# Attention's matmuls dealt out one by one from a template, on one Trainium2 core

## The chip, the core and the metric

The kernel runs on one NeuronCore of a Trainium2 chip. TensorE (PE in the profile) does the matrix products and the transpositions. Before each matmul it loads the stationary operand, a step that the profile keeps as an engine of its own (PEld). VectorE (DVE), ScalarE (ACT) and GpSimd (POOL) do the elementwise work. SyncE (SP) and ACT issue the DMAs. Each engine works through its instructions in a fixed order and waits on semaphores for the others. The metric is the device time of one execution in microseconds, lower is better.

## The reference

One transformer block in float32: x has 2048 rows of 1024. The attention has 32 heads of 32 columns and works on four segments of 512 rows; beside the causal softmax inside a segment it reads a memory M, z that sums up the earlier segments.

```python
for s in range(N):                                     # N = 4 segments of L = 512 rows
    qs, ks, vs = q[:, :, s], k[:, :, s], v[:, :, s]
    logits = jnp.einsum("bhqd,bhkd->bhqk", qs, ks) * scale + mask
    p = _softmax(logits, axis=-1)
    a_dot = jnp.einsum("bhqk,bhkd->bhqd", p, vs)
    pq = phi(qs)
    num = jnp.einsum("bhld,bhde->bhle", pq, M)
    den = jnp.einsum("bhld,bhd->bhl", pq, z)[..., None] + 1e-6
    o = g * (num / den) + (1.0 - g) * a_dot
    pk = phi(ks)
    M = M + jnp.einsum("bhld,bhle->bhde", pk, vs)
    z = z + jnp.einsum("bhld->bhd", pk)
...
h = x + _A_ref(_layernorm(x), ...)                     # the above, then times wo
h2 = h + _B_ref(_layernorm(h), ...)                    # gelu(y @ w1 + b1) @ w2 + b2, 3584 wide
```

## The kernel before

The rows are done in two halves of 1024. Each half runs the attention on two segments, then the product with `wo`, the second LayerNorm and the MLP. The MLP and all of its order are the same in both kernels.

Float32 accuracy is bought with split operands: each float32 value is a high part in fp32r and a low part (the rest), and a product is three matmuls, high by high, high by low and low by high. The low parts are made by subtractions on DVE and POOL.

**A unit** is one group of four heads (`g`, eight of them) in one segment (`sl`, two in a half): 16 units in a half. Its work on PE:

- The dense products: `kps`, `qps`, `vps`, each 8 chunks of 3 matmuls (L114 to L116), 72 matmuls with 128 columns of weights and 512 moving columns. The weights of a group are split by `weights` and `load_block`: the low part `wl` is a subtraction on POOL (L91).
- For each of its four heads: four score products `pqk` (L523, 128 to 512 moving columns), ten 128x128 transpositions `ppt` of the probabilities (L555), and eight products with the values, `po` (L575, 128 to 512 moving columns, only 64 columns of weights). I call these PV.
- The memory: transpositions `pkn`, `vn` and `pom` (four each), twelve products `pm` that read the memory (L386, 132 moving columns) and twelve products `pmm` that update it (L386, 128 columns). The first segment has no `pm` and `pom`, the last no `pmm` and `pkn`.

Between these stand DVE (the row minimum L524, the reciprocal L536, the low parts `ptl` L562), ACT (the exponential L532, the high parts `pth` L557) and POOL (the scaling of the probabilities `pr`, L539).

**What sets the order.** The program is written with generators. `dense` makes the dense products of one unit and yields after each chunk of three matmuls. `heads(prev)` makes the heads of the unit before, and `interleave` takes a step of the one and a step of the other. A head is a `slot` of six steps, written in `PLAN`: a letter is an operation and its digit a part, so `q1` is the score product of row block 1, `n0` the scaling of row blocks 0 and 1, `t0` the first group of four transpositions, `s0` its low parts, `a0` four PV matmuls, `o` the output. The letters work on three heads at a time: the present one (q, n), the one before (t, s) and the one before that (a, o, S).

The memory products wait in a list `small`. `one_small` takes one of them; it is called ahead of each transposition in `ptr` and ahead of most PV matmuls in `av`, so that a small product stands between two transpositions. The rest of a unit's memory work (`vn`, the filling of the list, `pom`) is in `late`, which runs in the next unit's dense part. A planner then takes this written order as priorities, and chooses each engine's final order from what it holds to be ready; in the MLP the written order is kept instead.

At the end of a half, the last unit's heads run beside the first `wo` products (`wo_first`), again by `interleave`, with the rates RA, RH and RS.

Of the kernel before, what the change touches and what calls it, by code (L numbers as in the profile page):

```python
# [16 lines left out]
P = 128  # L17
# [25 lines left out]
def build(tc, x, wq, wk, wv, wo, beta, w1, b1, w2, b2, out):  # L43
# [292 lines left out]
    def attention(half, first):  # L336
# [56 lines left out]
        def dense(g, sl, ws, u):  # L393
            s = 2 * half + sl
            behind = acts.pop("late", iter(()))
            kps = ws.pop("kps", None)
            if kps is None:
                kps = ps_dense("kps")
                for c in project(ws["k"], sl, "kps", kps):
                    if c >= 2:  # L400
                        next(behind, None)
                    yield
# [5 lines left out]
            for c in project(ws["q"], sl, "qps", qps):  # L408
                if c == 0:
                    nc.vector.tensor_tensor(kl, kps, raw(kh), op=ALU.subtract)  # L410
                    u["ks"] = stack(kh, kl, "ks", (0, 1, 0))
                if c == 2 and s < 3:
                    zc = ab.tile([P, 64], F32, name="zc", bufs=2)[:, 0:1]
                    pk = phi_sum(kparts, "pk", zc)
                next(behind, None)
                yield
# [4 lines left out]

            vps = ps_dense("vps")
            for c in project(ws["v"], sl, "vps", vps):
                if c == 0:
                    nc.vector.tensor_tensor(ql, qps, raw(qh), op=ALU.subtract)
                    u["qs"] = stack(qh, ql, "qs", (0, 0, 1))
                if s > 0:
                    if c == 2:
                        pq = phi_sum(qparts, "pq")
                    if c == 4:  # L430
                        while small:
                            one_small()
                        pqh, pql = tmpr("pqh"), tmpr("pql")
                        mzh = ab.tile([P, 256], F32R, name="mzh", bufs=1)[:, 0:132]
                        mzl = ab.tile([P, 256], F32R, name="mzl", bufs=1)[:, 0:132]
                        nc.scalar.copy(pqh, pq)
                        nc.vector.tensor_copy(mzh, MZ[:, g, :])
                        nc.gpsimd.tensor_tensor(mzl, MZ[:, g, :], raw(mzh), op=ALU.subtract)
                    if c == 5:
                        nc.gpsimd.tensor_tensor(pql, pq, raw(pqh), op=ALU.subtract)  # L440
                if c == 1 and s < 3:
                    pkn = ps_dense("pkn")
                    for i in range(4):
                        nc.tensor.transpose(pkn[:, i * P:(i + 1) * P], pk[:, i * P:(i + 1) * P], ident)
                    pkh, pkl = tmpr("pkh"), tmpr("pkl")
                    nc.scalar.copy(pkh, pkn)
                if c == 2 and s < 3:
                    nc.vector.tensor_tensor(pkl, pkn, raw(pkh), op=ALU.subtract)
                next(behind, None)
# [7 lines left out]
            def late():  # L457
                vn = ps_dense("vn")
                for c in range(4):
                    nc.tensor.transpose(vn[:, c * P:(c + 1) * P], vt[:, c * P:(c + 1) * P], ident)  # L460
# [3 lines left out]
                yield  # L464
                if s > 0:
                    om = tmp("om")

                    def memory(i2, ps):
                        pm = ps.rearrange("p (a b) -> p a b", a=2)
                        rg = ab.tile([P, 2, 32], F32, name="rg", bufs=2)[:, :, 0:4]  # L470
                        nc.vector.tensor_scalar(rg, pm[:, :, 128:132], DEN_EPS, None, op0=ALU.add)
                        nc.vector.reciprocal(rg, rg)
                        nc.vector.tensor_tensor(rg, rg, gate[:, 0:1, 4 * g:4 * g + 4].to_broadcast([P, 2, 4]), op=ALU.mult)
                        nc.vector.tensor_tensor(
                            om[:, i2 * 256:(i2 + 1) * 256].rearrange("p (a h e) -> p a h e", a=2, h=4),
                            pm[:, :, 0:128].rearrange("p a (h e) -> p a h e", h=4),
                            rg.unsqueeze(3).to_broadcast([P, 2, 4, DH]), op=ALU.mult)

                    for i2 in range(2):
                        smalls("pm", [(lambda ps, ii=ii: ps[:, 256 * ii:256 * ii + 132],  # L480
                                       pqh[:, (2 * i2 + ii) * P:(2 * i2 + ii + 1) * P],
                                       pql[:, (2 * i2 + ii) * P:(2 * i2 + ii + 1) * P], mzh, mzl, True, True)
                                      for ii in range(2)], partial(memory, i2))
                left = len(small)
                if s < 3:
                    def update(pmm):
                        for j in range(4):
                            b = slice(32 * j, 32 * j + 32)
                            nc.vector.tensor_tensor(MZ[b, g, b], pmm[b, b], MZ[b, g, b], op=ALU.add)
                        nc.vector.scalar_tensor_tensor(MZ[:, g, 128:132], hsel, zc, MZ[:, g, 128:132], op0=ALU.mult, op1=ALU.add)  # L490

                    smalls("pmm", [(lambda ps: ps[:, 0:P].rearrange("p (a b) -> p a b", a=4),
                                    pkh[:, c * P:(c + 1) * P], pkl[:, c * P:(c + 1) * P],
                                    vs[:, 4 * c:4 * c + 4, 0:32], vs[:, 4 * c:4 * c + 4, 32:64], c == 0, c == 3)
                                   for c in range(4)], update)
                total = len(small)
                while len(small) > total - left:
                    yield
                yield
                if s > 0:  # L500
                    pom = ps_dense("pom")
                    for i in range(4):
                        one_small()
                        nc.tensor.transpose(pom[:, i * P:(i + 1) * P], om[:, i * P:(i + 1) * P], ident)
                    nc.scalar.copy(omt, pom)  # L505
                while small:
                    yield
            for _ in behind:
                one_small()
            acts["late"] = late()  # L510
# [31 lines left out]
        def ptr(st, n):  # L542
            grp = ((0,), (1, 3), (2,))[n]
            if n == 0:
# [3 lines left out]
            ppt = psum.tile([P, 512], F32, tag="pt", name="ppt", bufs=2)  # L548
            base = koff[grp[0]]
            w = 0  # L550
            for jk in grp:
                for i in range(jk, 4):
                    one_small()
                    o = koff[jk] - base + (i - jk) * P
# [843 lines left out]
```

## Time and profile before

| | us |
|---|---|
| median of 3 runs (2356.2 to 2359.72) | 2358.24 |
| span of the profiled execution | 2354.0 |
| median less span (what lies around the instructions, and the difference of executions) | 4.2 |

| stretch of the span | what runs | PE busy |
|---|---|---|
| 0 to 60 us | the opening, first units | 46.27 of 60 |
| 60 to 530 us | attention of the first half | 455.27 of 470 |
| 950 to 1400 us | attention of the second half | 443.57 of 450 |
| the rest | `wo`, LayerNorm, MLP | not touched by the change beyond `wo_first` |

Matmuls are pipelined: the time given for one includes its way through the array, and the next starts before it ends. So a busy PE may still wait. How long a matmul really holds PE is read from the timeline, as the distance from its start to the start of the next. A matmul of 512 columns that follows another stands 0.23 us from the next. The timeline's columns are start, length, engine, line, operation, names, shape and count.

### The profile page before, as it was taken

The numbers are of one execution on the slowest core, as the hardware profiler recorded it, in microseconds if no ns is written. First come the engines' busy times: TensorE is split into PE (matmuls) and PEld (weight loads), VectorE is DVE, ScalarE is ACT, GpSimd is POOL, SyncE is SP. The second block draws the span as 40 slices with busy tenths as digits, with TensorE's granted clock in tenths as the row PEclk, the third lists the DMA queues.
The fourth block names the chain that finished last, engine by engine and source line by source line (L and its number), as shares of the span: only waits on it lengthen the run. The fifth ranks groups of instructions, "written<-read, shape, count | busy, mean of one in ns | idle before, by whom it ended". The sixth has DMA issues, their size and how long they took to land.

```text
span 2354.0 us, 35355 instructions
## 1 busy us (share of the span) xinstructions
PE 2288.6 (97%) x11769; PEld 1893.4 (80%) x11769; DVE 1575.9 (67%) x3334; ACT 1228.8 (52%) x2557; POOL 1058.4 (45%) x1037
## 2 busy tenths in 40 slices
PE   7999999999999999999999999999999999999999
PEld 6888888878878887888888877778887888888887
DVE  6777777776655565777777777564566676566753
ACT  5676776785453444777777776363343233222321
POOL 4444444445243442555555545252444564255430
PEclk9999999999999999999999999999999999999999
DMA  5333333345365654433333334466557976576762
GB/s 172 95 89 91 86 81 87 83 115 174 127 196 171 192 161 137 124 83 84 88 83 85 89 93 132 152 198 175 168 176 251 341 254 204 160 251 222 255 219 94
DMA packets 322719, 355.36 MB, mean 151 GB/s; under 512 B 26190, under 2 KB 218730, under 8 KB 322538
## 3 DMA queue, kind: packets, MB, share of 16 engines
q1 hardware_dynamic: 259370, 316.40, 44.7%
q10 hardware_dynamic: 63168, 36.71, 5.2%
q8 instruction: 93, 1.52, 0.3%
q14 instruction: 88, 0.72, 0.1%
HBM read 226.59 MB, written 76.09 MB: 129 GB/s over the span
## 4 chain that ended last, share of the span: by engine, by line
PE 73%; DVE 9%; ACT 7%; DMA 4%; POOL 3%; issue 3%; SPq 1%; ACTq 0%; POOLq 0%; DVEq 0%
PE po L1235 21%; PE bps L856 8%; PE dps L856 5%; PE ppt L555 5%; PE po L575 4%; PE cps L856 4%; PE pqk L523 3%; PE kps L114 2%; PE kps L115 2%; PE kps L116 2%; PE vps L114 2%; PE vps L115 2%; PE vps L116 2%; PE qps L114 2%; PE qps L115 2%
## 5 line engine op out<-in xcount | busy, mean ns | idle before, releaser
L539 POOL TENSOR_SCALAR pr<-pr,nm,gate 128x128 f32<-128x128 f32 (+3 forms) x512 | 320.9, 636 | 400.6 <-DVE nm L536 293.1
L532 ACT ACTIVATE pr<-pr,mx 128x256 f32<-128x256 f32 (+3 forms) x512 | 287.6, 562 | 179.1 <-DVE mx L524 176.5
L524 DVE CUSTOM_DVE_ANT_0 pr<-pqk,mask 128x256 f32<-128x256 f32 (+3 forms) x512 | 243.5, 484 | 37.7 <-PE pqk L523 35.2
L562 DVE TENSOR_TENSOR ptl<-ppt,pth 128x512 fp32r<-128x512 f32 (+1 forms) x384 | 227.2, 597 | 59.5 <-ACT pth L557 57.4
L555 PE MATMUL ppt<-ident,pr 128*128 128x128 f32 x1280 | 223.2, 277 | 1.8 <-DVE ptl L562 1.8
L557 ACT CAST pth<-ppt 128x512 fp32r<-128x512 f32 (+1 forms) x384 | 194.0, 518 | 42.3 <-PE ppt L555 36.7
L1245 DVE TENSOR_TENSOR c<-c,po 128x512 f32<-128x512 f32 x160 | 105.3, 683 | 146.1 <-PE po L1235 146.1
L555 PEld LDWEIGHTS ppt<-ident,pr 128*128 128x128 f32 x1280 | 164.4, 140 | 32.1 <-DVE ptl L562 3.6
L91 POOL TENSOR_TENSOR wl<-wr,wh 128x1024 fp32r<-128x1024 f32 x53 | 126.8, 2392 | 90.8 <-DVE wh L88 31.0
L523 PE MATMUL pqk<-ks,qs 96*128 96x256 f32 (+3 forms) x512 | 163.3, 320 | 1.6 <-DVE mx L524 1.6
L575 PE MATMUL po<-ptl,vs 128*64 128x512 f32 (+3 forms) x512 | 154.8, 312 | 5.9 <-DVE ptl L562 5.7
L575 PE MATMUL po<-pth,vs 128*64 128x512 f32 (+3 forms) x512 | 156.3, 327 | 2.2 <-ACT pth L557 2.1
L1235 PE MATMUL po<-w2h,zh 128*128 128x512 f32 x378 | 120.8, 389 | 0.0
L523 PEld LDWEIGHTS pqk<-ks,qs 96*128 96x128 f32 x512 | 96.6, 189 | 27.1 <-DVE mx L524 7.0
L536 DVE RECIPROCAL nm<-mx 128x2 f32<-128x2 f32 x256 | 42.2, 165 | 109.0 <-ACT pr L532 108.7
L968 POOL TENSOR_TENSOR s<-r 128x512 f32<-128x512 f32 x28 | 43.1, 1540 | 158.9 <-DVE sa L984 117.6
L1105 POOL TENSOR_TENSOR w2r<-w2r 128x512 f32<-128x512 f32 x54 | 85.4, 1593 | 62.3 <-DMA w2r<-in_B_w 62.3
L856 PE MATMUL bps<-zh,sa 128*128 128x512 f32 x336 | 110.7, 390 | 1.6 <-DVE u L998 1.6
L856 PE MATMUL bps<-zh,sb 128*128 128x512 f32 x336 | 111.0, 391 | 0.9 <-DVE u L1010 0.9
L114 PE MATMUL kps<-yh,wh 128*128 128x512 f32 (+1 forms) x264 | 110.2, 417 | 0.6 <-ACT yh L144 0.6
L114 PE MATMUL vps<-yh,wh 128*128 128x512 f32 x256 | 109.0, 426 | 0.2 <-ACT omt L505 0.2
L114 PE MATMUL qps<-yh,wh 128*128 128x512 f32 x256 | 106.8, 417 | 0.0
(237 smaller groups left out, 6748.0 us busy)
## 6 DMA issues: line engine op xcount, KB each, us to landing
hr<-h_dram SPq DMA_DIRECT2D x112, 448.0 KB, 4.8
w2r<-in_B_w SPq DMA_DIRECT2D x122, 256.0 KB, 4.4
r<-in_B_w SPq DMA_DIRECT2D x56, 512.0 KB, 4.6
h_dram<-ht ACTq DMA_DIRECT2D x84, 256.0 KB, 3.8
ks<-kh SPq DMA_DIRECT2D x256, 64.0 KB, 2.0
qs<-qh SPq DMA_DIRECT2D x256, 64.0 KB, 2.0
wr<-in_A_wo SPq DMA_DIRECT2D x32, 512.0 KB, 4.0
wx<-in_B_w SPq DMA_DIRECT2D x56, 256.0 KB, 3.7
```

The costliest lines, as they stand in the source:

```text
L114: nc.tensor.matmul(ps, ah, bh, start=first, stop=False)
L115: nc.tensor.matmul(ps, ah, bl, start=False, stop=False)
L523: nc.tensor.matmul(pqk[:, :n], u["qs"][j][:, i * P:(i + 1) * P], u["ks"][j][:, 0:n], start=True, stop=True)
L524: nc.vector.tensor_tensor_reduce(out=st["pr"][:, offs[i]:offs[i] + n], in0=pqk[:, :n], in1=mask[:, 512 - n:512], op0=ALU.add, op1=ALU.min, ...
L532: nc.scalar.activation(pi, pi, AF.Exp, bias=mx[:, i:i + 1], scale=-1.0, accum_out=mx[:, 4 + i:5 + i])
L539: nc.gpsimd.tensor_scalar(pi, pi, nm[:, 4 + k:5 + k], gate[:, 1, 4 * g + j:4 * g + j + 1], op0=ALU.mult, op1=ALU.mult)
L555: nc.tensor.transpose(ppt[:, o:o + P], pr[:, offs[i] + jk * P:offs[i] + (jk + 1) * P], ident)
L557: nc.scalar.copy(pth[:, base:base + w], ppt[:, :w])
L562: nc.vector.tensor_tensor(o, x0, x1, op=ALU.subtract)
L575: nc.tensor.matmul(po[:, P * jk:], v, st[part][:, koff[jk]:koff[jk] + w], start=(jk, part) == (0, "pth"), stop=(jk, part) == (2, "ptl"))
L856: nc.tensor.matmul(ps, x_[:, c, :], y_[:, c, :], start=first and c == 0 and n == 0, stop=last and c == 3 and n == 2, skip_group_check=True)
L1235: nc.tensor.matmul(ps, x_[:, k], y_[k], start=opens and k == 0 and i == 0, stop=closes and k == self.KP - 1 and i == 2, skip_group_check=True)
```

## The change

The dense products, the transpositions, the PV products and the memory products are now dealt out one matmul at a time.

- `project` yields after each matmul instead of after three.
- `PLAN` becomes a row of 60 marks for a head: D is one step of the dense products (20 of them), m is one item of `small` (12), and the operations are cut into single matmuls: `t00` to `t03` are the four transpositions of group 0, `ah0` and `al0` the PV products of key block 0 with the high and the low part. Four heads have 80 D for the 72 dense matmuls of a unit, so the last 8 find none.
- `ptr` and `av` make one matmul per call and no longer call `one_small`.
- `late` is gone. The transpositions `pkn`, `vn` and `pom` become four items of `small` each (`turned`), the split of the memory (`memories`) one more; all are put into the list in order, and the marks m take them.
- `wo_block` yields after each of its three matmuls; RH (14 to 42) and the rates of the other `interleave` calls are changed to the finer step. RA and RS stay.

The number of instructions on each engine and of each kind is the same in both programs; only the order differs. The planner still chooses each engine's order from the written one.

```diff
-RA, RH, RS, PD, PS = 1.3, 14, 0.7, 20, 3
-PLAN = ('q1 S2', 'q0 n0 a0', 'q2 t0 a1', 'q3 n2 s0 o', 't1', 's1 t2')
+RA, RH, RS, PD, PS = 1.3, 42, 0.7, 20, 3
+PLAN = ('q1 D S2 m D q0 D m ah0 n0 m al0 m ah1 m al1 t00 D t01 D t02 D t03 q2 s0 D ah3 D al3 D m ah2 m al2 q3 o '
+        't10 D t11 D t12 D t13 n2 D m D s1 t20 D t21 D m D m D m D m D').split()
...
             for c in range(DC):
-                mm3(ps, w[0][:, c, :], w[1][:, c, :], yh[:, c, :], yl[:, c, :], c == 0, c == DC - 1)
-                yield c
+                ops = ((w[0], yh), (w[0], yl), (w[1], yh))
+                for n, (a, b) in enumerate(ops):
+                    nc.tensor.matmul(ps, a[:, c, :], b[:, c, :], start=c == 0 and n == 0, stop=c == DC - 1 and n == 2)
+                    yield 3 * c + n
...
+            def turned(src, name, last):
+                ps = []
+
+                def one(i):
+                    if not ps:
+                        ps.append(ps_dense(name))
+                    nc.tensor.transpose(ps[0][:, i * P:(i + 1) * P], src[:, i * P:(i + 1) * P], ident)
+                    if i == 3:
+                        last(ps[0])
+
+                small.extend(partial(one, i) for i in range(4))
...
-            def late():
-                vn = ps_dense("vn")
-                for c in range(4):
-                    nc.tensor.transpose(vn[:, c * P:(c + 1) * P], vt[:, c * P:(c + 1) * P], ident)
+            def values(vn):
                 vn3 = vn.rearrange("p (a b) -> p a b", b=DH)
                 nc.scalar.copy(vs[:, :, 0:32], vn3)
                 nc.vector.tensor_tensor(vs[:, :, 32:64], vn3, raw(vs[:, :, 0:32]), op=ALU.subtract)
...
+                small.append(memories)
+            turned(vt, "vn", values)
...
-            for jk in grp:
-                for i in range(jk, 4):
-                    one_small()
-                    o = koff[jk] - base + (i - jk) * P
-                    nc.tensor.transpose(ppt[:, o:o + P], pr[:, offs[i] + jk * P:offs[i] + (jk + 1) * P], ident)
+            parts = [(jk, q) for jk in grp for q in range(jk, 4)]
+            jk, q = parts[i]
+            o = koff[jk] - base + (q - jk) * P
+            nc.tensor.transpose(ppt[:, o:o + P], pr[:, offs[q] + jk * P:offs[q] + (jk + 1) * P], ident)
...
-            for jk in (0, 1) if n == 0 else (3, 2):
-                w = 512 - P * jk
-                v = u["vs"][:, 4 * jk + j, :]
-                for part in ("pth", "ptl"):
-                    if (jk, part) != (3, "ptl"):
-                        one_small()
-                    nc.tensor.matmul(po[:, P * jk:], v, st[part][:, koff[jk]:koff[jk] + w],
+            w = 512 - P * jk
+            nc.tensor.matmul(po[:, P * jk:], u["vs"][:, 4 * jk + j, :], st["pt" + part][:, koff[jk]:koff[jk] + w],
...
-            for step in PLAN:
-                for op in step.split():
-                    call(ops[op[0]][0], ops[op[0]][1], *[int(c) for c in op[1:]])
-                yield
+            for op in PLAN:
+                if op == "D":
+                    yield
+                elif op == "m":
+                    one_small()
+                else:
+                    call(ops[op[0]][0], ops[op[0]][1], *[int(c) if c.isdigit() else c for c in op[1:]])
```

Three places show what this makes of the engines' orders. The first is PE in the middle of the `qps` products of a unit in the first half, where the memory products `pmm` of the unit before are due. Before:

```order
L115 MATMUL qps<-yl_191,wh 128x512
L116 MATMUL qps<-yh_190,wl 128x512
L386 MATMUL pmm<-vs,pkl 128x128
L504 MATMUL pom<-ident,om 128x128
L386 MATMUL pmm<-vs,pkh 128x128
L504 MATMUL pom<-ident,om 128x128
L386 MATMUL pmm<-vs,pkh 128x128
L504 MATMUL pom<-ident,om 128x128
L386 MATMUL pmm<-vs,pkl 128x128
L504 MATMUL pom<-ident,om 128x128
L386 MATMUL pmm<-vs,pkh 128x128
L555 MATMUL ppt<-ident,pr 128x128
```

After, in the same products:

```order
L352 MATMUL qps<-yh_190,wh 128x512
L389 MATMUL pmm<-vs,pkh 128x128
L352 MATMUL qps<-yl_191,wh 128x512
L549 MATMUL ppt<-ident,pr 128x128
L352 MATMUL qps<-yh_190,wl 128x512
L549 MATMUL ppt<-ident,pr 128x128
L352 MATMUL qps<-yh_190,wh 128x512
L389 MATMUL pmm<-vs,pkl 128x128
L352 MATMUL qps<-yl_191,wh 128x512
L389 MATMUL pmm<-vs,pkh 128x128
L352 MATMUL qps<-yh_190,wl 128x512
L389 MATMUL pmm<-vs,pkh 128x128
```

A `pmm` was followed by a transposition, and the run as a whole stood between two dense products; now each `pmm` and each transposition stands alone between two dense matmuls.

The second place is PE where a head's PV products of the last key block (128 moving columns) stand. Before:

```order
L523 MATMUL pqk<-ks,qs 128x384
L555 MATMUL ppt<-ident,pr 128x128 x4
L575 MATMUL po<-pth,vs 64x128
L575 MATMUL po<-ptl,vs 64x128
L575 MATMUL po<-pth,vs 64x256
L575 MATMUL po<-ptl,vs 64x256
L114 MATMUL qps<-yh_190,wh 128x512
```

After:

```order
L517 MATMUL pqk<-ks,qs 128x384
L352 MATMUL qps<-yh_190,wh 128x512
L565 MATMUL po<-pth,vs 64x128
L352 MATMUL qps<-yl_191,wh 128x512
L565 MATMUL po<-ptl,vs 64x128
L352 MATMUL qps<-yh_190,wl 128x512
L389 MATMUL pmm<-vs,pkl 128x128
L565 MATMUL po<-pth,vs 64x256
```

The four PV products were together; now the two short ones are each followed by a dense matmul.

The third place is POOL, in a unit that also splits the next group's weights (`wl`), with the scalings `pr` of its heads (the number is the row block's width). Before:

```order
L91 TENSOR_TENSOR wl<-wr,wh 128x1024
L539 TENSOR_SCALAR pr<-pr,nm,gate 128x384
L539 TENSOR_SCALAR pr<-pr,nm,gate 128x512
L440 TENSOR_TENSOR pql<-pq,pqh 128x512
L539 TENSOR_SCALAR pr<-pr,nm,gate 128x128
L539 TENSOR_SCALAR pr<-pr,nm,gate 128x256
L539 TENSOR_SCALAR pr<-pr,nm,gate 128x384
L539 TENSOR_SCALAR pr<-pr,nm,gate 128x512
L91 TENSOR_TENSOR wl<-wr,wh 128x1024
```

After:

```order
L92 TENSOR_TENSOR wl<-wr,wh 128x1024
L533 TENSOR_SCALAR pr<-pr,nm,gate 128x384
L533 TENSOR_SCALAR pr<-pr,nm,gate 128x512
L469 TENSOR_TENSOR pql<-pq,pqh 128x512
L533 TENSOR_SCALAR pr<-pr,nm,gate 128x128
L533 TENSOR_SCALAR pr<-pr,nm,gate 128x256
L92 TENSOR_TENSOR wl<-wr,wh 128x1024
L533 TENSOR_SCALAR pr<-pr,nm,gate 128x384
L533 TENSOR_SCALAR pr<-pr,nm,gate 128x512
```

The third split of the group has moved ahead of the scaling of a head's two widest row blocks, which stood ahead of it.

More of the change, by code (lines that the diff above doesn't have):

```diff
@@ L484, in late @@
[L484 to L502, printed above, removed]
-                        one_small()
[L504 to L509, printed above, removed]
@@ L646, in last @@
         def last():
-            behind = acts.pop("late")
-            for _ in chain(heads(prev), tail()):
-                next(behind, None)
-                yield
-            for _ in behind:
+            yield from chain(heads(prev), tail())
+            while small:
                 one_small()
@@ L697, in wo_block @@
             wh, wl = wts[n, g // 2]
-            mm3(ps, oh[:, g, cols], ol[:, g, cols], wh[:, g % 2], wl[:, g % 2], g == 0, g == NG - 1)
+            ops = ((oh, wh), (oh, wl), (ol, wh))
+            for n_, (a, b) in enumerate(ops):
+                acts["mm"] = nc.tensor.matmul(ps, a[:, g, cols], b[:, g % 2], start=g == 0 and n_ == 0,
+                                              stop=g == NG - 1 and n_ == 2)
+                if n_ < 2:
+                    yield "part"
             next(extra, None)
```

129 lines of the change are left out of this document (65 added, 64 removed).

## The prediction

> **What bounds the kernel now.** I read the page first, its engines and the chain that ended last.
>
> ```profile
> span 2354.0 us, 35355 instructions
> PE 2288.6 (97%) x11769; PEld 1893.4 (80%) x11769; DVE 1575.9 (67%) x3334; ACT 1228.8 (52%) x2557; POOL 1058.4 (45%) x1037
> PE 73%; DVE 9%; ACT 7%; DMA 4%; POOL 3%; issue 3%; SPq 1%; ACTq 0%; POOLq 0%; DVEq 0%
> ```
>
> PE is busy 97% of the span and carries 73% of the chain. So time is gained or lost on PE in two ways only: in its waits, or in how tightly its matmuls follow each other. The windows of the two attention stages, which the change touches, say how much there is in the waits.
>
> ```profile
> 60.00:530.00 470.00, 455.27 (x2751) 380.75 (x2749) 354.00 (x1082) 335.93 (x849) 224.93 (x283) 1.00 0.35 91
> 950.00:1400.00 450.00, 443.57 (x2692) 371.63 (x2691) 348.98 (x1069) 323.45 (x819) 235.19 (x295) 1.00 0.35 90
> ```
>
> The first number behind the stretch is PE's busy time: 14.7 us idle in the first half and 6.4 in the second, 21 us together, at a granted clock of 1.00. The chain of waits, for PE alone, names them (first half, then second):
>
> ```profile
> PE pmm L386 <- DVE kl L410: 5.9, 7, 0.8
> PE po L575 <- DVE ptl L562: 4.2, 6, 0.7
> ...
> PE pom L504 <- DVE om L474: 2.6, 7, 0.5
> PE pqk L523 <- DVE mx L524: 1.4, 7, 0.2
> ```
>
> They are short waits of about one in a unit. So a better order can win at most some 21 us here. The rest is the spacing of matmuls, which the timeline shows.
>
> **A short matmul costs what stands behind it.** By "short" I mean the products with 128 or 132 moving columns: 288 `pm`, 288 `pmm`, 256 of `po` and 128 of `pqk`, 960 in all. First a place where `pqk` and `pm` meet PV products, in the first half:
>
> ```profile
> 145.28 0.39 PE L116 MATMUL kps<-yh,wl 128*128 128x512 f32 x1
> 145.52 0.22 PE L523 MATMUL pqk<-ks,qs 96*128 96x128 f32 x1
> 145.58 0.28 PE L386 MATMUL pm<-mzh,pqh 128*128 128x132 f32 x1
> 145.69 0.39 PE L575 MATMUL po<-pth,vs 128*64 128x512 f32 x1
> 145.92 0.22 PE L386 MATMUL pm<-mzl,pqh 128*128 128x132 f32 x1
> 145.99 0.39 PE L575 MATMUL po<-ptl,vs 128*64 128x512 f32 x1
> 146.22 0.22 PE L386 MATMUL pm<-mzh,pql 128*128 128x132 f32 x1
> 146.28 0.34 PE L575 MATMUL po<-pth,vs 128*64 128x384 f32 x1
> ```
>
> A `pm` ahead of a `po` holds PE for 0.06 to 0.07 us (145.92 to 145.99, 146.22 to 146.28). But `pqk` and the `pm` behind it take 0.17 together (145.52 to 145.69) where twice 0.06 would be 0.12: 0.05 more. The two cases differ in the weights that must be loaded next, 64 columns for `po` and 128 for `pm`. Now one of the few places where a short product stands alone between two dense ones, as most will after the change:
>
> ```profile
> 941.66 0.39 PE L116 MATMUL kps<-yh,wl 128*128 128x512 f32 x1
> 941.89 0.22 PE L523 MATMUL pqk<-ks,qs 96*128 96x128 f32 x1
> 941.95 0.45 PE L114 MATMUL kps<-yh,wh 128*128 128x512 f32 x1
> 942.24 0.40 PE L115 MATMUL kps<-yl,wh 128*128 128x512 f32 x1
> ```
>
> From 941.66 to 942.24 are 0.58 us. Two dense matmuls at 0.23 make 0.46, so the short one cost 0.12, not 0.06. (The start of the dense one behind it reads 0.06 later, but that one then takes 0.29.) The weight loads, grouped by shape, give the reason:
>
> ```profile
> L575 PEld LDWEIGHTS po<-pth,vs 128*64 128x64 f32 x512 | 70.2, 137 | 18.0 <-ACT pth L557 4.1 <-issue 0.2
> L116 PEld LDWEIGHTS qps<-yh,wl 128*128 128x128 f32 x256 | 48.1, 188 | 11.0
> ```
>
> 64 columns more take 51 ns more, so a load of 128 columns occupies about 0.10 us and one of 64 about 0.05. The next load runs beside the present matmul. A dense matmul (0.23) hides any of them, a short one (0.06) hides 64 columns but not 128. So the price of a short product is 0.06 ahead of a `po` and, by the two places, 0.11 to 0.12 ahead of anything with 128 columns of weights: 0.055 more.
>
> What of a transposition? In the same run as the order's first place:
>
> ```profile
> 151.74 0.31 PE L386 MATMUL pmm<-vs,pkh 128*128 128x128 f32 x1
> 151.88 0.30 PE L504 MATMUL pom<-ident,om 128*128 128x128 f32 x1
> 151.93 0.31 PE L386 MATMUL pmm<-vs,pkh 128*128 128x128 f32 x1
> 152.07 0.30 PE L504 MATMUL pom<-ident,om 128*128 128x128 f32 x1
> 152.13 0.31 PE L386 MATMUL pmm<-vs,pkl 128*128 128x128 f32 x1
> ...
> 153.57 0.39 PE L116 MATMUL qps<-yh,wl 128*128 128x512 f32 x1
> 153.80 0.38 PE L555 MATMUL ppt<-ident,pr 128*128 128x128 f32 x2
> 153.94 0.48 PE L114 MATMUL qps<-yh,wh 128*128 128x512 f32 x1
> 154.25 0.40 PE L115 MATMUL qps<-yl,wh 128*128 128x512 f32 x1
> ```
>
> Two transpositions between dense matmuls: 0.68 us from 153.57 to 154.25, less 0.46, are 0.11 each. Four of them:
>
> ```profile
> 253.90 0.39 PE L116 MATMUL vps<-yh,wl 128*128 128x512 f32 x1
> 254.13 0.60 PE L555 MATMUL ppt<-ident,pr 128*128 128x128 f32 x4
> 254.49 0.48 PE L114 MATMUL vps<-yh,wh 128*128 128x512 f32 x1
> 254.81 0.40 PE L115 MATMUL vps<-yl,wh 128*128 128x512 f32 x1
> ```
>
> 0.91 less 0.46 is 0.45, again 0.11 each. A run of two costs no more for one than a run of four, so going in and out of a run is free, and a lone transposition should cost 0.11 as well. In the alternating run a pair of `pmm` and `pom` takes 0.195 (151.74, 151.93, 152.13). Less 0.11, a short product ahead of a transposition costs 0.085, 0.025 more than ahead of a `po`.
>
> **The change, part by part.** The instructions are the same in number and kind, so only places are priced. I counted in the two built orders what follows each of the 960 short products.
>
> - *A matmul with 128 columns of weights follows:* 77 times before, 676 after. 599 more at 0.055 us: +32.9. These are 161 `pm`, 169 `pmm`, 252 short `po` and 94 `pqk`.
> - *A transposition follows:* 384 times before, 33 after. 351 fewer at 0.025: -8.8.
> - *A `po` follows:* 499 before, 251 after, at the base price of 0.06.
> - *Lone transpositions:* one is followed by a dense matmul 312 times before and 1166 after. I price 854 more passages at nothing, since runs of two and four agree. They agree to 0.01 us, so the upper end is 854 x 0.01, 8.5 us.
> - *PE's waits, removed:* the item `pmm` waited for DVE since a whole run stood at one place. With one item every few matmuls most of such waits should end; the bounds are nothing and the 21 us above.
> - *PE's waits, added:* POOL's third `wl` of a group now stands ahead of the scaling of row blocks 2 and 3, which the next transpositions need. What that is worth, the present second split shows, which stands so already (two rows of POOL, one of PE):
>
> ```profile
> 254.46 2.39 POOL L91 TENSOR_TENSOR wl<-wr,wh 128x1024 fp32r<-128x1024 f32 x1 [0.76 <-issue]
> 256.92 1.77 POOL L539 TENSOR_SCALAR pr<-pr,nm,gate 128x384 f32<-128x384 f32 x2
> 259.28 0.60 PE L555 MATMUL ppt<-ident,pr 128*128 128x128 f32 x4
> ```
>
> The scaling ends at 258.69 and its transpositions begin at 259.28, so 0.59 us of slack are left there with the split ahead of it. Where the slack without the split is smaller, up to 2.39 - 0.59 = 1.8 us are added per group, 16 groups: 0 to 29 us. What is queued behind `wl` on POOL are the two `pr`; for them wait the transpositions on PE, and behind these everything on PE. I take removed and added waits as cancelling, since both are about one short wait in a unit, and keep both ends for the range.
> - *DMAs, SP's queue, `wo_first`:* the same issues; the rates per matmul are as before (three steps where there was one). Taken as nothing: DMA is busy 0.35 in both windows above.
>
> Sum: 32.9 - 8.8 = +24.1 us against the span of 2354.0. The median of the runs lies 4.2 us above that span, so the forecast is 2358.2 + 24.1 = 2382.3, 1.0% slower. About 0.2% (4.7 us) is what a measurement of this kernel can tell from no change.
>
> The Trainium skill, in "TensorE: Matmul & The Clock Gate", section "Back-to-back issue gap", gives a stream of load and matmul pairs with 128 columns about 81 ns each, one figure whatever stands behind. By it the first two terms would be nothing and the time 2358. The places above show 0.06 and 0.12 us for the same shape, so here the measurement decides against the single figure.
>
> **Rivals.**
> 1. *The loads stay hidden (faster).* If PE can load more than one set of weights ahead, the short product alone between dense ones costs 0.06. The same skill page, in "Step-by-step: what each phase is for", says that PE's reorder window pulls weight loads ahead of matmuls in flight. As a mechanism here: the +32.9 falls away, the -8.8 stays, and half the 21 us of waits go: 2358.2 - 8.8 - 10.5 = 2339. It decides from a price under 0.015 for each exposed load (599 x 0.015 = 8.8). For it speaks that lone short products are rare in this trace; against it are the one shown and the `pqk` and `pm` pair. Chance 0.08.
> 2. *The waits shrink as PE slows.* Each unit gets longer by 24.1/32 = 0.75 us on PE, and DVE, ACT and POOL do the same work in more time. If all 21 us of waits vanish, 2358.2 + 24.1 - 21 = 2361. Against it: waits end in chains from PE to ACT and DVE and back, and those chains are not shorter. Chance 0.10.
> 3. *POOL's split becomes the wait.* The 29 us come on top of the 24.1: 2411. For it speaks the slack of only 0.59 us; against it that only one of three splits moves. Chance 0.12.
>
> The forecast has 0.70. The range is 2362 to 2402: it reaches into rivals 2 and 3, half of each, and leaves out rival 1, so a little under 0.2 lies outside. The likeliest case alone spans 2372 to 2394, from its prices: 0.05 and 0.06 instead of 0.055, the 8.5 us of lone transpositions above, a few us of waits to either side. Faster 0.09 (rival 1, and a little of 2), same 0.07 (most of 2), slower 0.84.
>
> **What the new profile would show.** In the attention windows: short products ahead of dense ones with 0.06 to their follower's start and 0.28 or more from there to the next; lone transpositions at 0.11; PE's busy share as high as now or higher, since exposed loads do not show as idle time of 150 ns; each unit longer by some 0.75 us; the `wo`, LayerNorm and MLP stages shifted but equally long. A wait of `ppt` for POOL's `pr` should appear with a few tenths of a us. I am wrong if short products between dense matmuls stand at 0.29 us with their follower in one sum (0.06 + 0.23), or if PE's list of waits grows by more than 20 us.

## The result, and the profile after

| | before | after |
|---|---|---|
| median of 4 runs each | 2357.22 us | 2392.47 us |
| ratio of the times, with its 95% interval | | 1.0143 [1.0125, 1.0161] |
| span of the profiled execution | 2354.0 us | 2392.8 us |

The change made the kernel slower by 1.4%. The medians differ by 35.2 us; the ratio, taken run against run, gives 0.0143 x 2358 = 33.7. All differences below are taken from ratios to the kernel before, times 2358, because each group of runs had its own runs of that kernel beside it. The interval of the ratio makes 33.7 a figure of some 4 us to either side, and a difference of two ratios below is good to some 5 us. The forecast was +24.1 us, 2382; the range 2362 to 2402 holds the time.

The first lines of the page after, its engines and the chain that ended last:

```profile
span 2392.8 us, 35524 instructions
PE 2325.3 (97%) x11769; PEld 1883.0 (79%) x11769; DVE 1582.4 (66%) x3334; ACT 1223.3 (51%) x2557; POOL 1074.2 (45%) x1037
PE 78%; DVE 5%; POOL 5%; ACT 5%; DMA 4%; issue 3%; SPq 0%; ACTq 0%; POOLq 0%; DVEq 0%
```

The number of matmuls is the same, PE's share is the same 97%, and PE is 36.7 us busier. So a look at the shares alone would find nothing: the loss is counted as work. PE carries more of the chain (78% for 73%) and DVE less (5% for 9%).

The stretches of fifteen whole units, from the last matmul of a half's first `vps` product to the last of its sixteenth, show where it went. They hold the same matmuls in both kernels but for eight transpositions more after. Before, first and second half:

```profile
38.10:518.10 480.00, 465.31 (x2798) 389.67 (x2797) 357.69 (x1096) 336.81 (x858) 225.46 (x285) 1.00 0.35 90
938.70:1411.30 472.60, 464.95 (x2802) 388.32 (x2802) 363.63 (x1112) 340.57 (x862) 246.99 (x307) 1.00 0.35 91
```

After (columns: the stretch, its length, then PE, PEld, DVE, ACT and POOL busy, the granted clock, the DMA share, GB/s):

```profile
39.60:531.40 491.80, 481.54 (x2801) 383.22 (x2799) 357.33 (x1093) 333.40 (x857) 228.89 (x283) 1.00 0.34 88
959.70:1447.70 488.00, 479.41 (x2808) 384.04 (x2806) 360.76 (x1112) 338.46 (x862) 251.46 (x307) 1.00 0.35 88
```

Thirty units went from 952.6 to 979.8 us: 27.2 us, 0.9 for a unit. PE's idle time in them fell, from 22.3 to 18.8 us. The clock, the DMA share and the work of the other engines hardly moved. The two profiled spans differ by 38.8, so 11.6 us lie outside the thirty units: 1.5 in the opening, 7.7 between the two stretches (4.6 to the end of `wo`, 3.1 in an MLP whose order is the same in both kernels) and 2.4 behind the second (0.3 and 2.1). Some 3 of them are the executions' own: that of after was the slowest of its four, 2.1 us above their median, and that of before lay about 1 us under its median. The granted clock has a part in that: between the two stretches it stood at 0.50 for 10.2 us after (536.6 to 540.0 and 693.6 to 700.4) and for 3.4 us before (677.1 to 680.5), which is worth up to 3.4 us.

The short products in the timeline of after, PE, first half: a `pm` alone between dense matmuls, and the PV products of the last key block at the order's second place.

```profile
147.37 0.22 PE L389 MATMUL pm<-mzh,pqh 128*128 128x132 f32 x1
147.43 0.44 PE L352 MATMUL kps<-yh,wh 128*128 128x512 f32 x1
147.71 0.22 PE L389 MATMUL pm<-mzl,pqh 128*128 128x132 f32 x1
147.77 0.44 PE L352 MATMUL kps<-yl,wh 128*128 128x512 f32 x1
148.05 0.22 PE L389 MATMUL pm<-mzh,pql 128*128 128x132 f32 x1
...
151.83 0.39 PE L352 MATMUL qps<-yh,wh 128*128 128x512 f32 x1
152.06 0.22 PE L565 MATMUL po<-pth,vs 128*64 128x128 f32 x1
152.12 0.45 PE L352 MATMUL qps<-yl,wh 128*128 128x512 f32 x1
152.41 0.22 PE L565 MATMUL po<-ptl,vs 128*64 128x128 f32 x1
152.47 0.45 PE L352 MATMUL qps<-yh,wl 128*128 128x512 f32 x1
```

From one `pm` to the next are 0.34 us, and from one short `po` to the next 0.35. Less 0.23 for the dense matmul, each short product holds PE for 0.11 to 0.12, where the same `po` ahead of another `po` held it for 0.06. As forecast, the start of the follower reads 0.06 and the cost shows up as 0.28 to 0.29 behind the follower.

The lone transpositions, a little later:

```profile
153.36 0.27 PE L549 MATMUL ppt<-ident,pr 128*128 128x128 f32 x1
153.39 0.48 PE L352 MATMUL qps<-yh,wh 128*128 128x512 f32 x1
153.71 0.27 PE L549 MATMUL ppt<-ident,pr 128*128 128x128 f32 x1
153.74 0.48 PE L352 MATMUL qps<-yl,wh 128*128 128x512 f32 x1
154.05 0.27 PE L549 MATMUL ppt<-ident,pr 128*128 128x128 f32 x1
```

0.69 us for two of them with two dense matmuls: 0.345 less 0.23 is 0.115 each, not 0.11.

PE's list of waits after, the one line that is new and large:

```profile
PE ppt L549 <- POOL pr L533: 11.4, 29, 0.7
```

And the largest waits of the attention before, of which 1.8 us are left (1.1 of `pom`, 0.7 of `po`):

```profile
PE pmm L386 <- DVE kl L410: 6.9, 8, 1.0
...
PE po L575 <- DVE ptl L562: 5.7, 13, 0.7
...
PE pom L504 <- DVE om L474: 3.0, 8, 0.5
```

One of the new waits, where POOL's third `wl` stands ahead of the scaling that the transpositions need (POOL, then PE):

```profile
138.87 2.41 POOL L92 TENSOR_TENSOR wl<-wr,wh 128x1024 fp32r<-128x1024 f32 x1 [3.06 <-PE vn L427]
141.25 2.39 POOL L533 TENSOR_SCALAR pr<-pr,nm,gate 128x384 f32<-128x384 f32 x4
```

```profile
140.57 0.47 PE L352 MATMUL kps<-yl,wh 128*128 128x512 f32 x1
140.88 0.27 PE L549 MATMUL ppt<-ident,pr 128*128 128x128 f32 x1
140.91 0.48 PE L352 MATMUL kps<-yh,wl 128*128 128x512 f32 x1
141.98 0.33 PE L549 MATMUL ppt<-ident,pr 128*128 128x128 f32 x1 [0.59 <-POOL pr L533]
142.06 0.48 PE L352 MATMUL kps<-yh,wh 128*128 128x512 f32 x1
142.73 0.33 PE L549 MATMUL ppt<-ident,pr 128*128 128x128 f32 x1 [0.19 <-POOL pr L533]
```

From a dense matmul to the transposition behind it are 0.31 us without a wait (140.57 to 140.88). Here it is 1.07 and 0.67. So 0.76 and 0.36 were lost where the list has 0.59 and 0.19: each wait takes some 0.17 us more than is listed, since the matmul ahead of it still counts as busy. For 29 waits that is an estimated 11.4 + 29 x 0.17 = 16 us.

### The profile page after: what moved, and what is told of

It reads as the page before. It is cut to its first block, busy times and chain, and to the rows that moved or that the text cites. A ratio compares the mean times of both kernels' runs of the same rounds, so it can differ in the third digit from the quotient of the medians.

```text
span 2392.8 us, 35524 instructions
## 1 busy us (share of the span) xinstructions
PE 2325.3 (97%) x11769; PEld 1883.0 (79%) x11769; DVE 1582.4 (66%) x3334; ACT 1223.3 (51%) x2557; POOL 1074.2 (45%) x1037
## 4 chain that ended last, share of the span: by engine, by line
PE 78%; DVE 5%; POOL 5%; ACT 5%; DMA 4%; issue 3%; SPq 0%; ACTq 0%; POOLq 0%; DVEq 0%
PE po L1230 20%; PE bps L851 8%; PE vps L352 7%; PE qps L352 7%; PE kps L352 7%; PE po L565 5%; PE dps L851 5%; PE ppt L549 5%; PE pwo L690 4%; PE cps L851 4%; PE pqk L517 3%; POOL wl L92 1%; POOL pr L533 1%; PE pmm L389 1%; ACT vt L450 1%
## 5 line engine op out<-in xcount | busy, mean ns | idle before, releaser
L549 PE MATMUL ppt<-ident,pr 128*128 128x128 f32 x1280 | 332.3, 274 | 12.3 <-POOL pr L533 11.4
L552 ACT CAST pth<-ppt 128x512 fp32r<-128x512 f32 (+1 forms) x384 | 187.4, 517 | 108.1 <-PE ppt L549 104.9
L549 PEld LDWEIGHTS ppt<-ident,pr 128*128 128x128 f32 x1280 | 178.0, 141 | 29.9 <-POOL pr L533 20.8
L92 POOL TENSOR_TENSOR wl<-wr,wh 128x1024 fp32r<-128x1024 f32 x53 | 127.3, 2402 | 111.8 <-PE vn L427 43.1
L565 PE MATMUL po<-pth,vs 128*64 128x512 f32 (+3 forms) x512 | 164.1, 321 | 2.6 <-DVE ot L576 1.3
L565 PE MATMUL po<-ptl,vs 128*64 128x512 f32 (+3 forms) x512 | 162.2, 317 | 0.8 <-DVE ptl L557 0.7
L352 PE MATMUL qps<-yh,wh 128*128 128x512 f32 x256 | 115.7, 452 | 1.1 <-DVE om L482 0.6
L352 PE MATMUL vps<-yh,wl 128*128 128x512 f32 x256 | 115.8, 452 | 0.0
L352 PE MATMUL qps<-yl,wh 128*128 128x512 f32 x256 | 114.3, 446 | 0.0
L352 PE MATMUL qps<-yh,wl 128*128 128x512 f32 x256 | 113.5, 444 | 0.0
L352 PE MATMUL vps<-yl,wh 128*128 128x512 f32 x256 | 113.2, 442 | 0.0
```

Source lines behind the costliest of these rows:

```text
L92: getattr(nc, lo_eng).tensor_tensor(lo, w, raw(hi), op=ALU.subtract)
L352: nc.tensor.matmul(ps, a[:, c, :], b[:, c, :], start=c == 0 and n == 0, stop=c == DC - 1 and n == 2)
L549: nc.tensor.transpose(ppt[:, o:o + P], pr[:, offs[q] + jk * P:offs[q] + (jk + 1) * P], ident)
L552: nc.scalar.copy(pth[:, base:base + w], ppt[:, :w])
L565: nc.tensor.matmul(po[:, P * jk:], u["vs"][:, 4 * jk + j, :], st["pt" + part][:, koff[jk]:koff[jk] + w], start=(part, jk) == ("h", 0), sto ...
```

## Experiments

My theory: the loss is mainly the 128-column weight loads that stand behind short products, at about 0.055 us each; the rest is waits. The rivals were POOL's split as the main cause, and a price that adds up from moving columns and load instead of being set by the longer of the two. I counted for every built order how many of the 960 short products stand ahead of 128 columns of weights, of a transposition and of a `po`: 77 / 384 / 499 before, 676 / 33 / 251 after.

**e1: the PV products of the last key blocks put together again.** The changed kernel, with the marks `ah3` and `al3` moved out from between the dense ones, to stand ahead of `ah2`:

```diff
-... q2 s0 D ah3 D al3 D m ah2 m al2 q3 o
+... q2 s0 D D D m ah3 al3 ah2 m al2 q3 o
```

The counts become 424 / 33 / 503: 252 loads less to be waited for. The transpositions keep their places.

> Changed kernel with one edit of the template: the short PV products of a head (128 moving columns) stand together again and ahead of the wider PV pair. In the built order short products followed by 128 columns of weights fall from 676 to 424; those followed by a transposition stay at 33. Theory (exposed weight loads, 0.055 us each): 252 x 0.055 = 13.9 us less than the changed kernel's 2392.5, so 2378 to 2379. Rival (the loss is in new waits, above all POOL's): within 3 us of 2392.

Measured: 1.0090 [1.0075, 1.0105], 12.5 us less than after: 0.050 for a load, with some 0.02 to either side. The timeline of this kernel, first half, PE:

```profile
152.24 0.22 PE L564 MATMUL po<-pth,vs 128*64 128x128 f32 x1
152.30 0.22 PE L564 MATMUL po<-ptl,vs 128*64 128x128 f32 x1
152.36 0.28 PE L564 MATMUL po<-pth,vs 128*64 128x256 f32 x1
```

Ahead of 64 columns of weights the same two products stand 0.06 apart. Moving two marks of PLAN gave back more than a third of the loss.

**e2: `pm` made wider.** The changed kernel; `pm` moves 228 columns instead of 132 (the 96 further ones belong to the next group's memory, and what is made of them is not read):

```diff
-                mzh = ab.tile([P, 256], F32R, name="mzh", bufs=1)[:, 0:132]
-                mzl = ab.tile([P, 256], F32R, name="mzl", bufs=1)[:, 0:132]
+                mzh = ab.tile([P, 256], F32R, name="mzh", bufs=1)[:, 0:228]
+                mzl = ab.tile([P, 256], F32R, name="mzl", bufs=1)[:, 0:228]
...
-                    nc.vector.tensor_copy(mzh, MZ[:, g, :])
-                    nc.gpsimd.tensor_tensor(mzl, MZ[:, g, :], raw(mzh), op=ALU.subtract)
+                    wide = acts["mz"][:, 132 * g:132 * g + 228]
+                    nc.vector.tensor_copy(mzh, wide)
+                    nc.gpsimd.tensor_tensor(mzl, wide, raw(mzh), op=ALU.subtract)
```

> Changed kernel with the 288 pm products widened from 132 to 228 moving columns (the added columns are of the next group's memory and are not read). 228 columns stream in about 0.10 us, still less than the 0.11 of a 128-column load. Theory (a lone short product is bound by the next load): the 161 pm ahead of a 128-column load cost nothing more, the 126 ahead of a po cost 0.04 more: +5 us, 2397; the distance between dense matmuls round a lone pm stays at 0.34 to 0.35. Rival (each change between short and dense has a fixed price on top of the columns): +288 x 0.04 = 11.5 us, 2404, and the distance grows to 0.38.

Measured: 1.0186 [1.0164, 1.0209], 10.1 us more than after. The total is nearer the rival's number, so by it alone the theory would have lost. But the place itself, in the same products as shown of after, decides otherwise:

```profile
148.35 0.40 PE L352 MATMUL kps<-yh,wl 128*128 128x512 f32 x1
148.59 0.28 PE L389 MATMUL pm<-mzh,pqh 128*128 128x228 f32 x1
148.70 0.40 PE L352 MATMUL kps<-yh,wh 128*128 128x512 f32 x1
148.93 0.27 PE L389 MATMUL pm<-mzl,pqh 128*128 128x228 f32 x1
149.04 0.40 PE L352 MATMUL kps<-yl,wh 128*128 128x512 f32 x1
149.27 0.27 PE L389 MATMUL pm<-mzh,pql 128*128 128x228 f32 x1
```

From one `pm` to the next are 0.34 us, as with 132 columns. Nor is this place alone: at the 69 places of each trace where two `pm` stand round one dense matmul without a wait, the median distance is 0.344 us in both kernels. So 96 more columns cost nothing there, as it has to be if the load of the next weights takes as long anyway. The rival needs 0.38. Only the 126 `pm` that stand ahead of a `po` became dearer, by about 0.04, which makes some 5 us. Of the other 5 us a part is seen as a wait that the wider split brought on, in the stretch from 900 to 1600 us:

```profile
PE pom L427 <- DVE om L483: 3.7, 8, 1.8
...
PE qps L352 <- DVE om L483: 1.3, 1, 1.3
```

After has 1.1 us of the first there and none of the second.

**e8: the other direction, in the kernel before.** The short products of the last key block are put last instead of first among a head's PV products, so that dense weights follow them:

```diff
-            for jk in (0, 1) if n == 0 else (3, 2):
+            for jk in (0, 1) if n == 0 else (2, 3):
...
-                                     start=(jk, part) == (0, "pth"), stop=(jk, part) == (2, "ptl"))
+                                     start=(jk, part) == (0, "pth"), stop=(jk, part) == (3, "ptl"))
```

The counts become 190 / 383 / 387: 113 more exposed loads.

> Kernel before with one edit in av: the PV products of key block 3 (128 moving columns) come behind those of block 2, so the last one is followed by a dense matmul instead of a wider PV product. Counted in the built order: 190 short products ahead of 128 columns of weights instead of 77, 387 ahead of a po instead of 499; nothing else moves. Theory (exposed loads, 0.055 us each): +113 x 0.055 = +6.2 us, ratio 1.0026. Rival (the price comes with the fine template or its waits, not with the load): 1.000.

Measured: 1.0021 [1.0009, 1.0033], 5.0 us more, 0.044 for a load, with some 0.025 to either side. Its timeline:

```profile
157.05 0.22 PE L575 MATMUL po<-pth,vs 128*64 128x128 f32 x1
157.11 0.22 PE L575 MATMUL po<-ptl,vs 128*64 128x128 f32 x1
157.16 0.44 PE L114 MATMUL qps<-yh,wh 128*128 128x512 f32 x1
157.45 0.39 PE L115 MATMUL qps<-yl,wh 128*128 128x512 f32 x1
```

0.06 from the first short product to the second, but 0.34 from the second past its dense follower. The price holds in the old order too, with none of the template's other effects. How far the total is made of it is less sure: 101 of the 113 loads lie in the thirty units, which became only 1.9 us longer in the profile, with PE's listed waits there 2.6 us shorter.

**e3: one of POOL's three splits taken away.** The changed kernel; the low part of the weights for `vps` is made on DVE:

```diff
-                ws[n] = load_block(wp, w, g * P, 3, "vector" if g or n == "k" else "scalar")
+                ws[n] = load_block(wp, w, g * P, 3, "vector" if g or n == "k" else "scalar", "vector" if g and n == "v" else "gpsimd")
```

> Changed kernel with the low part of the v weights (one of three splits of a group, from the second group on) made by DVE instead of POOL. Theory (exposed loads): the waits of ppt for POOL's pr, 11.4 us idle in the list, fall by more than half, DVE is a little later elsewhere: 0 to 10 us less than 2392.5, and most of the 35 us loss stays. Rival 3 (POOL's split is the main cause): 20 us or more less, 2372 or lower.

Measured: 1.0106 [1.0089, 1.0123], 8.7 us less than after. The waits for POOL are nearly gone, some for DVE have come:

```profile
PE po L565 <- DVE ptl L557: 6.3, 16, 0.4
...
PE ppt L549 <- POOL pr L533: 0.9, 2, 0.7
```

So POOL's split is a part of the loss and not its main cause; with only two splits left on POOL the kernel still is 25 us slower than before.

**e4: a template with few exposed loads.** A new PLAN for the changed kernel, in which transpositions and short products again stand beside each other:

```diff
-PLAN = ('q1 D S2 m D q0 D m ah0 n0 m al0 m ah1 m al1 t00 D t01 D t02 D t03 q2 s0 D ah3 D al3 D m ah2 m al2 q3 o '
-        't10 D t11 D t12 D t13 n2 D m D s1 t20 D t21 D m D m D m D m D').split()
+PLAN = ('q1 D S2 D q0 ah0 n0 m al0 m ah1 m al1 D D t00 m t01 m t02 m t03 D D q2 s0 D D m ah3 al3 ah2 m al2 q3 o '
+        'D D t10 m t11 m t12 m t13 n2 D D s1 D t20 m t21 D D D D D D D').split()
```

The counts become 82 / 276 / 602, nearly those of before.

> Changed kernel with a template, still one matmul at a time, that puts each short product ahead of a PV product or between two transpositions. Counted in its order: 82 short products ahead of 128 columns of weights (676 in the changed kernel, 77 in the one before), 276 ahead of a transposition (33, 384). Theory (exposed loads): -594 x 0.055 + 243 x 0.025 = -26.6 us, so about 2366, if the waits stay as in the changed kernel. Rival (waits): the template's fineness costs by itself, the time stays above 2385.

Measured: 1.0084 [1.0069, 1.0099], 13.9 us less than after where the prices gave 26.6. The expectation missed by half. What is late next stands in its list of waits:

```profile
PE ppt L548 <- POOL pr L532: 16.8, 32, 0.9
PE vn L426 <- ACT vt L449: 6.2, 23, 0.5
```

PE reaches the transpositions sooner and waits longer for POOL, and it now waits for ACT as well. In the thirty units by themselves hardly anything was won: 977.5 us against 979.8. So I cut POOL's long instruction.

**e6, e5, e7: POOL's split in two halves.** In all three, every `wl` of 128x1024 of the weights for `kps`, `qps` and `vps` is written as two subtractions of half the size, so that a scaling can go between them. e6 is the kernel before with this alone, e5 is e4 with it, and e7 is e5 with the `vps` split on DVE as in e3 (there 28 subtractions of half the size, not 14).

```diff
-        split(pool, wr, wh, wl, hi_eng, lo_eng)
+        split(pool, wr, wh, wl, hi_eng, None)
+        for k in (slice(0, 4), slice(4, 8)):
+            getattr(nc, lo_eng).tensor_tensor(wl[:, k], wr[:, k], raw(wh)[:, k], op=ALU.subtract)
```

> Kernel before with each attention split wl on POOL made in two halves of 1.28 us. PE does not wait for POOL there, so no gain is expected: ratio 1.000, within 0.002. If POOL's long instruction delayed PE in a way the list of waits does not show, it would be 0.996 or lower.

> The template with short products ahead of PV (ratio 1.0084 to the kernel before), with each wl on POOL in two halves. Its list shows 16.7 us of idle time of ppt for POOL's pr, against 11.4 in the changed kernel and 0 before. Theory (with the loads covered, that wait is most of what is left): half or more of it goes, 8 to 17 us, ratio 1.001 to 1.005. Rival (other waits of the template take over): 1.007 or more.

> As the run before it in this list, and the v weights' low part on DVE from the second group on. Theory: the waits of ppt for POOL nearly vanish, 15 to 20 us less than with the template alone, ratio 1.000 to 1.002; if also below 0.998 it beats both kernels. Rival: DVE, with 14 more subtractions, delays PE as much as POOL did, ratio 1.005 or more.

Measured: e6 1.0007 [0.9994, 1.0021]; e5 0.9995 [0.9984, 1.0006]; e7 0.9975 [0.9963, 0.9987]. The halves do nothing for the kernel before. On e4's template they give back 21 us, more than I expected, and e7 is 6 us (3 to 9) faster than the kernel before, the best version here. The waits of e7, to be set against e4's:

```profile
PE vn L429 <- ACT vt L452: 5.9, 23, 0.5
PE ppt L551 <- POOL pr L535: 1.5, 4, 0.8
```

From e4 to e7 the listed wait falls by 15.3 us. With the 0.17 us that each of the 28 waits takes beyond the list that makes 20.1, of 25.7 measured. The other 5.6 us have no line of their own.

**e9 and e10: the same splits in the kernel before and under the changed kernel's own template.** e9 is the kernel before and e10 the changed kernel, each with the halves and the `vps` split on DVE; their diffs are those of e3 and e6 together.

> Kernel before with the same splits (wl in halves, the v weights' low part on DVE). PE waits for neither there; DVE gets 14 more subtractions. Expected 0.999 to 1.003. If it is 0.998 or less, the gain of the run that beat both comes from the splits and not from the template.

> Changed kernel, its own template, with the splits of the run that beat both (wl in halves, the v weights' low part on DVE). The waits of ppt for POOL should go as there, the 676 exposed loads stay. Theory (exposed loads cost 0.055 us each, POOL's wait the rest): the template with covered loads and the same splits measured 0.9975; -594 loads and +243 transpositions behind a short product are worth 26.6 us, so here 0.9975 + 0.0113 = 1.009, and 1.007 to 1.010 with 0.050 us for a load. Rival 3 (POOL's split is the main cause of the loss): 1.003 or less.

Measured: e9 1.0011 [0.9999, 1.0022]; e10 1.0087 [1.0069, 1.0105]. In e10 the waits for POOL's scaling are nearly gone; the largest wait of the attention that is left on PE is one for DVE, which had 1.1 us in after:

```profile
PE pom L430 <- DVE om L485: 5.1, 8, 1.1
...
PE po L568 <- DVE ot L579: 1.4, 4, 0.4
...
PE ppt L552 <- POOL pr L536: 0.9, 2, 0.7
```

Two things follow. e10 and e7 differ in the template alone: 0.0112 x 2358 = 26.4 us, for 594 exposed loads more and 243 short products fewer ahead of a transposition, which the prices put at 594 x 0.055 - 243 x 0.025 = 26.6 (30.2 with 0.005 us more for each of the 725 transpositions more that a dense matmul follows in e10). That the totals agree so closely is partly luck. In the thirty units alone e10 takes 18.3 us longer, where the prices with the 0.005 give 28.3; e7 has other waits there (for ACT's `vt` above all, 5.9 us in its list), and 6.1 more lie beside `wo`. And e9 shows that e7's gain does not come from the splits alone: they give nothing in the old order, 13.2 us under the changed template (after to e10), and 25.7 under the one with few exposed loads (e4 to e7).

## Why the prediction was right in its sign and mechanism, and 10 us short

The profiled executions, cut at the same matmuls, show where the loss lies (us):

| stretch | before | after | e9 | e10 | e4 | e7 |
|---|---|---|---|---|---|---|
| the opening | 38.1 | 39.6 | 38.3 | 39.6 | 39.0 | 39.1 |
| the thirty units | 952.6 | 979.8 | 952.2 | 968.3 | 977.5 | 950.0 |
| PE's listed waits in them | 22.0 in 47 | 16.0 in 37 | 22.6 in 47 | 9.3 in 16 | 29.6 in 61 | 12.9 in 33 |
| from there to the end of `wo`, both halves | 233.8 | 238.7 | 233.9 | 239.0 | 232.7 | 232.9 |
| the first half's MLP, to the end of the next half's first `vps` | 304.5 | 307.6 | 306.0 | 306.6 | 304.8 | 306.2 |
| the second half's MLP | 825.0 | 827.1 | 824.5 | 822.9 | 825.9 | 829.3 |

The opening, the thirty units and the two stretches beside `wo` are 1.5, 27.2 and 4.9 us longer after than before, 33.6 together, near the 33.7 of the ratio. The other 5.2 of the two spans' difference are in the MLP, and there kernels with one and the same order differ by as much.

- **Exposed loads, +32.9: right.** The price of 0.055 is what the distances show (0.11 to 0.12 against 0.06), and it came out as 0.050 (e1) and 0.044 (e8), both with wide bounds. The short product's own columns are not the cause: e2 made the product longer without making it dearer there. What stands behind it decides, as e1 and e8 show; no run changed the width of the next weights by itself, so that their load is the reason is read from the two widths of the traces. The Trainium skill, in "TensorE: Matmul & The Clock Gate", section "LDWEIGHTS (loading the stationary operand)", puts a load at its columns divided by 1.2 in ns, by which an estimate for 128 is 107 and for 64 is 53 ns. The trace agrees: a short product costs 0.11 to 0.12 us ahead of the one and 0.06 ahead of the other, though the 0.06 may as well be the product's own 128 columns (0.23 x 128/512 is 0.06). The single figure of 81 ns that the prediction weighed from the same page of the Trainium skill does not hold here.
- **Fewer short products ahead of a transposition, -8.8: only tested together with the loads,** in e10 less e7, and never by itself.
- **Lone transpositions at nothing: too low.** They take 0.115 and not 0.11. For the 854 passages that is an estimated 854 x 0.005 = 4.3 us, which the sum had at nothing; it is half of the upper end that the prediction kept. Placing them in runs again, and nothing else, was not tried.
- **Waits removed and added taken as cancelling: right in the sum, by luck.** In the thirty units lie 576 of the 599 loads, 347 of the 351 short products and 801 of the 854 transpositions: 31.7 - 8.7 + 4.0 = 27.0 us, and 27.2 were measured. So next to nothing is left there for the balance of the waits. Neither side of it was small. Without POOL's long split the new order makes the thirty units only 16.1 us longer (e9 to e10) where these prices give 27.0: some 11 us of old waits went, and PE's list has 13.3 less. The long split then brings 11.5 in the new order (e10 to after) and nothing in the old one (before and e9); by the ratios it is 13.2, by the list an estimated 16. The prediction named the place, the slack and the queue behind it, and set two terms with bounds of 21 and 29 us equal without working out either. That they met is luck.
- **Each unit +0.75 us: low.** Thirty whole units gained 27.2, 0.9 each.
- **`wo_first` and the opening at nothing: too low, and the cause stays open.** Beside `wo` the two stretches took 4.9 us more (after) and 5.1 more (e10 against e9), while e4's and e7's template takes no more there than the old order. The 23 exposed loads more outside the thirty units make 1.3 of it by the prices, and the clock at 0.50 from 536.6 to 540.0 us up to 1.7 in after, but e10 has no such stretch there. No run took `wo_first` apart. The opening is 1.5 us longer, for which no run has a reason either. Together with the transpositions these make up the 9.6 us (33.7 less 24.1), within what the ratio's interval allows.
- **DMAs and SP's queue at nothing:** the DMA share of the thirty units is 0.34 to 0.35 in both. **The MLP at nothing:** its two stretches are 5.2 us longer in the profile, no more than such executions differ.
- **Rival 1 (loads pulled ahead) falls.** A lone short product takes 0.34 to 0.35 us with its dense follower where the rival needs 0.29. **Rival 2 (waits vanish as PE slows)** is about half true: some 11 us of old waits went, whether because PE is slower or because the items stand apart no run tells. **Rival 3 (POOL's split)** is about half true as well: it exists, at 12 to 16 us and not 29. The two hid one another, so the time came out near the sum that left both away. (In rival 1, 599 x 0.015 is 9.0 and not 8.8; nothing hangs on it.)
- **Busy share as high as before: right.** 97% in both, with PE's idle time in the thirty units down by 3.5 us while they took 27.2 more.

## What to carry to other kernels

Before matmuls are interleaved, count for each short one what weights the next one loads: where the load takes longer than the moving columns, the difference is lost, so put short products ahead of matmuls with narrow weights, or side by side in runs that end in one. The loss does not show as idle time, so read start-to-start distances over a whole period. And when PE's order is tightened, look for long instructions of a helper engine ahead of what PE needs, and cut them: against the kernel before, here neither the new template with few exposed loads (e4, 20 us slower) nor the cut (e6 and e9, nothing) paid alone, while both together beat it (e7).

## What was unexpected about the hardware

Exposed loads and waits hide one another. The two templates differ by 13.9 us with POOL's long split in place (after to e4) and by 26.4 without it (e10 to e7), though the same loads were covered. In the thirty units alone the difference is 2.3 us with the split and 18.3 without, where the prices give 28.3 both times. With the split in place most of what was saved on loads went into waiting, and PE's list named only a part of that: it grew by 13.6 us in 24 more waits from after to e4, some 17.7 with the 0.17 us that the two waits shown run short.

A transposition alone between dense matmuls is dearer by about 0.005 us than one in a run (0.115 against 0.11), although going in and out of a run had looked free.
